# Two more pairs mixed with tokens on partitions, one unit more in the first batch, and one o stage a step forward

## Chip, cores and metric

One NeuronCore of a Trainium2 chip runs the whole kernel. The metric is the device time of one execution in microseconds, and a kernel is judged by several executions. Most executions of one kernel agree within some tenths of a per cent here, but single ones are 1 to 3% longer. Such a run is set aside as slow where it lies over 1.5% above the fastest of its kernel. Times inside a profile (start times, lengths) are counted from the start of the profiled execution, whose span is some 2 us shorter than its device time.

## The reference, cut to what matters

```python
# q, k, v: (B=4, H=8, S=768, D=64); sort_net: (B, H, 8, 8); block = 96
P = sort_net
for _ in range(5):                                   # Sinkhorn: rows and columns in turn
    P = exp(P - max(P)); P = P / rowsum; P = P / colsum
k_sorted = einsum('bhij,bhjcd->bhicd', P, k_b)       # mix the 8 blocks of 96 tokens
v_sorted = einsum('bhij,bhjcd->bhicd', P, v_b)
attn = softmax(q_b @ k_sorted_b.T / sqrt(D))         # within a block
x = (attn @ v_sorted_b)                              # -> (3072, 512), heads side by side
out = ((x @ w_a) * (x @ w_b)) @ w_out                # 512 -> 1536 -> 512
```

## The kernel before

Two heads make a pair; a batch has four pairs (`HP = 4`), so pairs 0 to 3 belong to the first batch, 4 to 7 to the second and so on to 15. The feed-forward part of one batch runs while the attention of the next is prepared between its steps. The attention is cut into units: `c` mixes k and v of a pair, `s` makes scores and exponentials, `o` multiplies with v and turns the result for the feed-forward part. Results of matmuls stand in buffers of a memory called PSUM (the pools `psA` and `psF`) until ScalarE or VectorE has copied them out. A unit stands in a list, and `paced` spreads the list of a batch evenly over the feed-forward steps (the first batch's list here has 18 steps, of about 1.3 us each).

There are two ways of mixing. The old one puts features on partitions at once and takes 24 half-array matmuls; the other leaves tokens on partitions, takes four full matmuls, and then has the DMA crossbar turn the result and GpSimd put it in order:

```python
def stage_k(g):                       # old way; stage_v is alike
    mix = psA.tile([P, 2, 512], FP32, tag="A", name="mix")
    ...
    mix_mms(g, "k", ...)              # 12 matmuls of 128x128, half the array each
    nc.scalar.copy(out=kTs[g % HP] in block order, in_=mix)

def plain(g):
    return g >= 2 * HP + 2            # pairs 10 to 15 take the other way

def stage_plain(g, what, engines):
    ...
    for e in range(2):
        nc.tensor.matmul(mix[:, e, 0:W], lhsT=s_all[:, 2 * g + e], rhs=src2[:, e], ...)
    ...                               # copies mix to nat (bf16)
    nc.sync.dma_start_transpose(out=turned, in_=nat...)     # the crossbar turn

def stage_q(g):                       # q is turned by the crossbar as well, for all pairs from 6 on
    qT = qtp.tile([P, NCH, P], BF16, tag="qTf", name="qTf", bufs=4)
    nc.sync.dma_start_transpose(out=qT, in_=st[g, "qc"]...)
    st[g, "qT"] = qT

def return_v(g):                      # and v back to tokens on partitions
    nc.sync.dma_start_transpose(out=vss[g % NBUF]..., in_=vTs[g % HP]...)
```

All these turns go through one queue, in the order in which they are asked for. Loads of k, v and q go through another; the loads of a later pair are asked for by GpSimd, and a one-element copy called a gate stands before them, so that GpSimd can't ask before something else is finished:

```python
def c_(g):
    ...
    else:                             # a pair mixed the old way
        if g > HP:
            return_v(g)
        if g >= 2 * HP - 2 and g != 2 * HP - 1:
            nc.gpsimd.tensor_copy(out=gate, in_=kTs[g % HP][0:1, 0:1])
            load_later(g)             # loads pair g + 2

def paced(ab, po, units, spare, last):
    steps = ab + po
    total = len(steps) - 2 * spare
    main, done = len(units) - last, 0
    for now, step in enumerate(steps, 1):
        step()
        while done < main and done * total < now * main:
            units[done]()
            done += 1
        ...
```

`c6` asks for the loads of pair 8 (k, v and q, 192 KB each), behind a gate on the k that `c6` itself has just mixed.

The softmax here doesn't subtract the row's maximum and nothing guards it: scores larger than these inputs give would overflow.

## Time and profile before

| | before |
|---|---|
| runs before the prediction | 239.97 us (239.78 to 241.39) |
| span of the profiled run | 238.2 us |
| TensorE busy | 231.5 us, 97% |

The engine shares, the chain and the DMA rows that carry the bound are in the prediction. The first view lists where TensorE waited (in all, times, the longest, in us); the start-up's rows are left out:

```profile
PE pf L362 <- DMA w_b_sb<-in_moe_w_b_dram: 0.5, 1, 0.5
...
PE o_ps L236 <- DVE xp L242: 0.2, 1, 0.2
```

The second is GpSimd's own timeline around the load of pair 8 (start, length, what; in brackets an idle time before it and what ended it):

```profile
50.49 3.96 POOL L153 TENSOR_TENSOR s_all<-mask,p_col 128x1024 bf16<-128x1024 bf16 x2
54.43 0.18 POOL L589 COPY gate<-kT 1x1 bf16<-1x1 bf16 x1
54.93 0.76 POOL L96 DMA_DIRECT2D k<-in_k_dram  x1 [0.32 <-PE pf L362]
```

The third has two transfers asked for at about that time (issued from a queue, how many, us from issue to landing): the turn of q of pair 7, asked for at 52.55, and the load of k of pair 8, asked for at 54.93.

```profile
qTf<-qc SPq DMA_TRANSPOSE x1, 9.5
...
k<-in_k_dram POOLq DMA_DIRECT2D x1, 192.0 KB, 7.8
```

The reader is to see that the load of pair 8 is asked for at 54.93, which is 2.4 us after the turn of q7, and that the turn takes 9.5 us and lands at 62.05. Score stage `s7` starts at 65.43 and doesn't wait for it.

### The profile page before, as it was taken

The numbers are of one execution on the slowest core, as the hardware profiler recorded it, in microseconds if no ns is written. First come the engines' busy times: TensorE is split into PE (matmuls) and PEld (weight loads), VectorE is DVE, ScalarE is ACT, GpSimd is POOL, SyncE is SP. The second block draws the span as 40 slices with busy tenths as digits, with TensorE's granted clock in tenths as the row PEclk, the third lists the DMA queues.
The fourth block names the chain that finished last, engine by engine and source line by source line (L and its number), as shares of the span: only waits on it lengthen the run. The fifth ranks groups of instructions, "written<-read, shape, count | busy, mean of one in ns | idle before, by whom it ended". The sixth has DMA issues, their size and how long they took to land.

```text
span 238.2 us, 5168 instructions
## 1 busy us (share of the span) xinstructions
PE 231.5 (97%) x2064; PEld 138.2 (58%) x2074; DVE 108.5 (46%) x256; ACT 101.4 (43%) x189; POOL 70.4 (30%) x97
## 2 busy tenths in 40 slices
PE   7999999999999999999999999999999999999994
PEld 7776566666554565666555465656554566565442
DVE  7795566546543333465415243645444243444110
ACT  3696543665430366554530366355500234333001
POOL 8786248765010355162420533420000000000000
PEclk9999999999999999999999999999999999999999
DMA  5999999999998999579996999970434300000132
GB/s 76 203 198 193 158 192 201 204 199 189 129 173 169 190 165 170 106 121 168 146 174 172 189 195 143 132 145 4 77 81 128 125 0 3 0 0 3 59 117 88
DMA packets 65703, 30.88 MB, mean 130 GB/s; under 512 B 42512, under 2 KB 62736, under 8 KB 65680
## 3 DMA queue, kind: packets, MB, share of 16 engines
q0 software_dynamic: 20944, 14.16, 42.8%
q1 hardware_dynamic: 44592, 16.33, 37.6%
q8 instruction: 16, 0.26, 0.5%
q10 hardware_dynamic: 144, 0.07, 0.1%
q14 instruction: 7, 0.06, 0.1%
HBM read 28.32 MB, written 6.29 MB: 145 GB/s over the span
## 4 chain that ended last, share of the span: by engine, by line
PE 86%; DMA 5%; DVE 4%; POOL 1%; issue 1%; ACT 1%; DVEq 0%
PE pf L362 51%; PE po L407 24%; DMA w_b_sb<-in_moe_w_b_dram 5%; PE o_ps L236 3%; PE sc L332 2%; PE mix L175 2%; PE mix L303 2%; PE po L392 1%; DMA p_nat<-in_sort_net_dram 1%; POOL w_a_sb L107 1%; DVE csum L461 1%; ACT p_nat L439 1%; DVE xp L242 1%; DVE p_nat L459 0%; POOL s_all L153 0%
## 5 line engine op out<-in xcount | busy, mean ns | idle before, releaser
L383 DVE TENSOR_TENSOR hT<-a_sb,pf 128x384 bf16<-128x384 bf16 x95 | 52.5, 553 | 73.8 <-PE pf L362 44.0
L362 PE MATMUL pf<-xT,w_a_sb 128*128 128x384 bf16 x380 | 78.0, 326 | 0.0
L362 PE MATMUL pf<-xT,w_b_sb 128*128 128x384 bf16 x380 | 77.5, 326 | 0.5 <-DMA w_b_sb<-in_moe_w_b_dram 0.5
L382 ACT CAST a_sb<-pf 128x384 bf16<-128x384 f32 x95 | 45.4, 479 | 61.2 <-PE pf L362 38.2
L407 PE MATMUL po<-w_out_sb,hT 128*128 128x512 bf16 x266 | 61.0, 379 | 0.5
L362 PEld LDWEIGHTS <-w_b_sb 128*128 128x128 bf16 x384 | 37.4, 98 | 25.6 <-DMA w_b_sb<-in_moe_w_b_dram 1.0
L362 PEld LDWEIGHTS <-w_a_sb 128*128 128x128 bf16 x384 | 35.3, 98 | 22.5
L407 PEld LDWEIGHTS <-hT 128*128 128x128 bf16 x276 | 26.3, 98 | 30.1
L161 ACT COPY o_sb<-po 128x512 f32<-128x512 f32 (+1 forms) x13 | 7.5, 577 | 48.9 <-PE po L407 47.5
L163 DVE COPY o_sb<-po 128x512 f32<-128x512 f32 (+1 forms) x12 | 7.9, 658 | 38.7 <-PE po L407 34.1
L337 ACT ACTIVATE eT<-sc 96x768 bf16<-96x768 f32 x24 | 18.0, 802 | 5.1 <-PE sc L332 5.0
L242 DVE TENSOR_TENSOR xp<-o_ps,rec 96x512 bf16<-96x512 f32 x24 | 15.9, 684 | 0.3
L319 POOL COPY kT<-turned 128x768 bf16<-128x768 bf16 x6 | 5.0, 826 | 35.6 <-DMA turned<-nat 31.2
L96 POOL DMA_DIRECT2D k<-in_k_dram x16 | 11.6, 724 | 4.9 <-DMA w_a_sb<-in_moe_w_a_dram 2.7
L96 POOL DMA_DIRECT2D v<-in_v_dram x16 | 11.5, 722 | 4.8 <-DMA w_b_sb<-in_moe_w_b_dram 3.1
L251 POOL COPY qc<-q 128x768 bf16<-128x768 bf16 x10 | 8.4, 841 | 13.8 <-DMA q<-in_q_dram 13.8
L236 PEld LDWEIGHTS <-eT 96*128 96x128 bf16 x256 | 10.3, 97 | 3.4 <-DVE xp L242 0.6
L236 PE MATMUL o_ps<-vs,eT 96*128 96x65 bf16 x256 | 11.3, 193 | 0.3 <-DVE xp L242 0.2
L161 ACT CAST nat<-mix 128x768 bf16<-128x768 f32 (+1 forms) x12 | 7.7, 638 | 4.2 <-PE mix L303 3.0
L96 POOL DMA_DIRECT2D q<-in_q_dram x12 | 8.7, 724 | 2.4 <-DMA w_a_sb<-in_moe_w_a_dram 1.2
L167 PE MATMUL heat<-warm 128*128 128x128 bf16 x84 | 7.8, 268 | 1.3 <-DVE warm L77 1.3
L240 DVE RECIPROCAL rec<-o_ps 96x8 f32<-96x8 f32 x32 | 5.5, 188 | 5.3 <-PE o_ps L236 5.3
(87 smaller groups left out, 154.1 us busy)
## 6 DMA issues: line engine op xcount, KB each, us to landing
out_dram<-o_sb SPq DMA_DIRECT2D x17, 256.0 KB, 2.2
k<-in_k_dram POOLq DMA_DIRECT2D x16, 192.0 KB, 5.9
v<-in_v_dram POOLq DMA_DIRECT2D x16, 192.0 KB, 6.6
q<-in_q_dram POOLq DMA_DIRECT2D x12, 192.0 KB, 7.4
w_a_sb<-in_moe_w_a_dram POOLq DMA_DIRECT2D x6, 256.0 KB, 10.6
w_b_sb<-in_moe_w_b_dram POOLq DMA_DIRECT2D x6, 256.0 KB, 12.1
w_out_sb<-in_moe_w_out_dram POOLq DMA_DIRECT2D x3, 512.0 KB, 11.2
out_dram<-o_sb SPq DMA_DIRECT2D x12, 128.0 KB, 2.8
```

The lines of the kernel that those rows point to most:

```text
L96: nc.gpsimd.dma_start(out=to, in_=_ap(t, base, [[W, P], [S * D, 2], [1, W]]))
L161: nc.scalar.copy(out=out, in_=in_)
L163: nc.vector.tensor_copy(out=out, in_=in_)
L167: nc.tensor.matmul(ps[:, 0:cols], lhsT=warm[:, 0:P], rhs=warm[:, 0:cols], start=True, stop=True)
L236: nc.tensor.matmul(o_ps[:, e, i * (D + 1):(i + 1) * (D + 1)], lhsT=eT[:, hf, e, i * BLK:i * BLK + P], rhs=vs[0:BLK, i0 + i, V0 - 1 + e * ( ...
L242: nc.vector.tensor_tensor(out=_ap(xp, i0 * 2 * D, [[nxp * 2 * D, BLK], [D, 2], [2 * D, NBH], [1, D]]), in0=_ap(o_ps, 1, [[1024, BLK], [511 ...
L251: nc.gpsimd.tensor_copy(out=qc.rearrange("p c e d -> p e c d"), in_=loaded[g][2].rearrange("p e (c d) -> p e c d", c=NCH))
L337: nc.scalar.activation(out=eT[:, hf, :, 0:HB], in_=sc[0:BLK, :, 0:HB], func=AF.Exp, scale=float(scale))
L362: nc.tensor.matmul(pf[:, 0:HW], lhsT=w_sb[:, kc, m * P:(m + 1) * P], rhs=x_cols(b, kc, t), start=(kc == 0), stop=(kc == KA - 1))
L382: nc.scalar.copy(out=a_sb, in_=pf[:, 0:HW])
L383: nc.vector.tensor_mul(out=hT[:, m, t * HW:(t + 1) * HW], in0=a_sb, in1=ab[1][:, 0:HW])
L407: nc.tensor.matmul(held["po"], lhsT=hTs[b][:, m, c * P:(c + 1) * P], rhs=w_out_sb[:, m, :], start=(m == 0), stop=(m == KO - 1))
```

## The change

The intent: pairs 8 and 9 are mixed the cheaper way too. Since the other way takes longer from mixing to use, `c8` is drawn into the first batch, and its v is returned at once; the loads of pairs 9 and 10 now wait for the last turned o stage of the second batch. Apart from that, the first o stage of the first batch's second half comes one step sooner.

```diff
     def plain(g):
-        return g >= 2 * HP + 2
+        return g >= 2 * HP
@@ c_
-                if g >= 2 * HP - 2 and g != 2 * HP - 1:
+                if g == 2 * HP - 2:
                     nc.gpsimd.tensor_copy(out=gate, in_=kTs[g % HP][0:1, 0:1])
                     load_later(g)
@@ o_
-            if g == 2 * HP - 1:
-                nc.gpsimd.tensor_copy(out=gate, in_=xT_of(g // HP)[0:1, HP - 1, 0:1])
-                load_later(g)
@@ the lists
-        plan(0, "c4", "s4", "c5", "s5", "c6", "o4", "s6", "c7", "o5", "s7", "o6", "o7")
-        plan(1, "c8", "s8", "c9", "s9", "c10", "o8", "c11", "o9", "s10", ...
+        plan(0, "c4", "s4", "c5", "s5", "c6", "o4", "s6", "c7", "o5", "s7", "o6", "c8", "o7")
+        plan(1, "s8", "c9", "o8", "c10", "s9", "c11", "o9", "s10", ...
@@ what follows a unit of the plain kind
+                if g == 2 * HP:
+                    after[n + 1].append(lambda g=g: return_v(g))
+                    after[n + 1] += [lambda g=g: nc.gpsimd.tensor_copy(
+                        out=gate, in_=xT_of(1)[0:1, HP - 1, 0:1]),
+                                     lambda g=g: load_later(g - 1), lambda g=g: load_later(g)]
+                    continue
@@ second half of the first batch
-        interleave(steps, units_half(), (0, 0, 1, 0, 1, 2, 1, 1, 1, 2, 1, 0))
+        interleave(steps, units_half(), (0, 0, 1, 1, 0, 2, 1, 1, 1, 2, 1, 0))
```

Thirteen units instead of twelve in the first list mean, through `paced`, that most units come a step sooner; the prediction gives the formula. `c6` is number 5 (counted from 0): it comes after step 7 instead of 8.

More of the change, by code (lines that the diff above doesn't have):

```diff
@@ L617, in plan @@
                 seq.append((b, {"c": c_, "s": s_, "o": o_}[name[0]], int(name[1:])))
-        plan(0, "c4", "s4", "c5", "s5", "c6", "o4", "s6", "c7", "o5", "s7", "o6", "o7")
-        plan(1, "c8", "s8", "c9", "s9", "c10", "o8", "c11", "o9", "s10", "c12", "s11", "o10", "o11",
+        plan(0, "c4", "s4", "c5", "s5", "c6", "o4", "s6", "c7", "o5", "s7", "o6", "c8", "o7")
+        plan(1, "s8", "c9", "o8", "c10", "s9", "c11", "o9", "s10", "c12", "s11", "o10", "o11",
              "c13")
```

## The prediction

> **What bounds the kernel now.** I read the page first (engine shares), then the chain of waits in order of time, then the DMA issues with their times to landing. The page says that TensorE is the bound:
>
> ```profile
> PE 231.5 (97%) x2064; PEld 138.2 (58%) x2074; DVE 108.5 (46%) x256; ACT 101.4 (43%) x189; POOL 70.4 (30%) x97
> PE 86%; DMA 5%; DVE 4%; POOL 1%; issue 1%; ACT 1%; DVEq 0%
> ```
>
> The first line is busy time by engine, the second the chain that ended last. From 27.7 us to the end that chain is one row of TensorE groups with almost nothing between them. So the time can only fall if TensorE gets fewer or cheaper groups, or if one of its few waits goes. The pieces that the change touches (start, length, group):
>
> ```profile
> 27.68 0.82 PE pf L362 x4
> 28.51 0.25 PE o_ps L236 x8
> 53.07 0.79 PE mix L175 x24
> 53.86 1.41 PE pf L362 x8
> 64.20 1.30 PE po L407 x6
> 65.50 0.30 PE sc L332 x8
> 68.89 0.69 DVE o_sb L163
> 69.77 1.26 DVE xp L242 x2
> 71.07 0.42 PE o_ps L236 x8
> 96.46 0.65 PE mix L303 x4
> 97.11 3.90 PE pf L362 x24
> ```
>
> The reader is to see three things. (1) A pair mixed the old way (24 half-array matmuls, L175) costs 0.79 us, and the eight feed-forward matmuls after it 1.41 us. A pair mixed with tokens on partitions (4 full matmuls, L303) costs 0.65, and the matmuls after it 3.90 for 24, that is 1.30 for eight. (2) At 69 to 71 us the chain leaves TensorE: the o stage of pair 7 waits for VectorE to empty PSUM. (3) At 27.68 TensorE has just waited for a weight load. The DMA issues beside this (the last number is us from issue to landing; each is from a narrow window at its issue):
>
> ```profile
> vs<-vT SPq DMA_TRANSPOSE x1, 11.8
> vs<-vT SPq DMA_TRANSPOSE x1, 8.2
> qTf<-qc SPq DMA_TRANSPOSE x1, 2.7
> v<-in_v_dram POOLq DMA_DIRECT2D x1, 192.0 KB, 10.4
> v<-in_v_dram POOLq DMA_DIRECT2D x1, 192.0 KB, 4.5
> ```
>
> They are: v of pair 6 returned, issued at 55.5 (lands 67.3); v of pair 7, issued at 62.15 (lands 70.35); q of pair 8 turned, issued at 69.8; v of pair 8 loaded, issued at 55.7 (lands 66.1); v of pair 9 loaded, issued at 78.0 (lands 82.5). A transfer takes two to four times as long before about 67 us as after it.
>
> **What the Trainium skill says.** "TensorE: Matmul & The Clock Gate", section "Back-to-back issue gap": a warm matmul takes N/2.4 + 2.5 ns. For 384 columns that is 162.5 ns, eight are 1.30 us; for 512 columns 215.8 ns, six are 1.30 us. The trace agrees to the digit (1.30 for eight, 1.30 for six), and four mixing matmuls of 384 columns come out at 0.65 as shown. "TensorEngine Tiling (Array Packing)", section "Key Properties": switching the tiling mode drains TensorE. The trace agrees: 1.41 - 1.30 = 0.11 us after each half-array group, and 0.79 against 12 x 53.3 ns = 0.64 us of streaming (two halves side by side) going in. "DMA: Bandwidth & Descriptors", section "Issuing engines are not separate DMA queues": all DMAs share the same 16 engines and interleave. The trace agrees: with loads running, turns take 8 to 12 us, otherwise 2.7.
>
> **The change part by part.**
> Part 1, the form of mixing of pairs 8 and 9. Each old group costs 0.79 + 0.11 = 0.90 us of TensorE, each new one 0.65. Two pairs: 2 x 0.25 = 0.50 us off the path, 40 matmuls fewer. ScalarE and VectorE empty the same PSUM in the same sizes (0.80, 0.56, 0.48 us each pair): nothing. GpSimd gets four reordering copies of 0.83 us = 3.3 us more and loses two gates, and it is 30% busy. The SP queue gets four more turns. What the path sees is only latency: mix to k ready is about 0.8 (ScalarE copy) + 2.7 (turn at a quiet time) + 0.8 (GpSimd) = 4.3 us, v and its return some 4 more.
>
> Part 2, c8 moves into the first batch. Thirteen units instead of twelve are spread over the same 18 steps, so unit k comes after step floor(18k/13)+1 instead of floor(1.5k)+1. Most units come one step (1.3 us) earlier: o5 after step 12 (was 13), s7 after 13 (was 14), o6 after 14 (was 16); c8 takes step 16 and o7 stays at 17. I place them on the old clock, where step 12 ends at 62.25.
> - o7 no longer follows o6 by one step. In its place come c8's PSUM copies, done about 1.9 us after c8 begins, before o7 wants them at about 2.0 to 2.2. The old wait (PSUM matmuls at 70.48 + 0.25 = 70.73, second half at 71.07) was 0.34 us: gained.
> - s7 follows o5, and o5 now comes right behind the last a-and-b product, whose VectorE product (62.54 to 63.10) stands before o5's reciprocal. Then 2 x (0.20 + 0.69) ends at 64.87, but s7's second half wants the buffer at 62.25 + 0.49 + 1.30 + 0.22 = 64.27: wait 0.6, where the old pair of small waits was 0.2. Lost: about 0.43 with what follows.
> - o6 then comes at 64.9 + 0.25 + 0.1 + 1.30 = 66.55. Its v lands at 67.3 in the old run. Its turn is asked for 0.8 us earlier in the new order (the SP queue stands back to back from 49.7 to 61.4), but its ring was also full of earlier turns and the loads of pair 8 drain until 67.4, so I give it only part of this: landing 66.5 to 67.3. Lost: 0 to 0.8 us, I take 0.4.
> - k and v of pair 8 land by 66.1 and c8 comes at about 69.6 or later: no wait. s8 wants its k at about 82.5, ready by 75: no wait.
>
> Part 3, the first o stage of the second half one step forward. It fills 0.25 us of the wait before 27.68. But the w_b piece for the next two steps lands at 17.86 + 13.0 = 30.86 us (its issue and time to landing), and the matmuls on it started at 30.96 already. So all but 0.03 us of it is waited for again three microseconds later. I count 0.03.
>
> Sum: -0.50 (form) - 0.34 (o7) + 0.43 (s7) + 0.40 (o6 on v6) - 0.03 (first o stage) = -0.04 us. With a little on the good side, since the orders were surely tuned by someone looking at these waits, I predict 239.8 us against 239.97.
>
> **The rivals.**
> Rival A: the waits of s7 and o6 don't come, because v6 lands with its earlier issue and VectorE is ahead. Then the sum is -0.50 - 0.34 - 0.03 = -0.87: 239.1. For it: one to two microseconds of slack are at stake in many places, and the ring of turns begins earlier. Against it: VectorE's order is fixed and the arithmetic for s7 leaves no room.
> Rival B: the turn of v6 takes as long as before from the same drain (67.4 us), or later since nothing else became lighter: +0.8 to +1.0 at o6, sum about +0.5: 240.5. For it: its 11.8 us end just where the loads of pair 8 end.
> Rival C: a wait on the load of pair 9 takes the place of all this. c9 comes after step 3 of the second batch instead of step 5, at about 85.6. The gate for its load stands on GpSimd behind two reordering copies and waits for the last xT of the first batch, which lands at about 77.6 (76.8 before). Then v9 is issued at 78.8 and lands with 4.5 us at 83.3: 2.3 us of slack. If the turns of pair 8 hold that xT up on the SP queue by over 2 us, or the six loads now issued together slow one another, c9 waits one or two microseconds: 241 to 242. Against it: loads issued first have landed first in every window that I read.
> Nothing here reaches 4.8 us, which is 2%.
>
> **Range and chances.** From the best case (239.1) to B (240.5), with 0.2 to 0.3 us for the scatter of the three runs (239.78 to 241.39 before): 238.9 to 240.8 holds it 8 times in 10. Faster by over 2% would need more than TensorE's whole idle time after 27 us, which the chain puts at under 2 us: 0.01. Slower by over 2% needs C and more: 0.02. Within 2%: 0.97.
>
> **What would show it right or wrong.** Part 1: mixing groups of 0.65 us for pairs 8 and 9 too, followed by 1.30 for eight and not 1.41; 24 k-matmuls and 24 v-matmuls fewer under L175. o7: no VectorE piece in the chain before its second half. s7: a wait of about 0.6 us for VectorE's xp before its second half. o6: a wait for the DMA into vs, or none if rival A holds. Part 3: a shorter wait for w_b near 27 us and a new one just before 31 us. Rival C: TensorE idle before the first L303 matmuls on k or v near 85 us. The prediction is wrong if TensorE's gaps between 62 and 72 us change by over 1 us in either direction, or if a gap opens after 80 us where I see none.

## The result

| | before | after |
|---|---|---|
| median of 6 runs | 240.01 us (239.78 to 241.98) | 243.74 us (242.91 to 245.24) |
| ratio of fast runs | | 1.0137 (1.0089 to 1.0184) |
| span of the profiled run | 238.2 us | 241.3 us |

A ratio is the mean time of one kernel's fast runs over that of the other's fast runs of the same rounds, so not quite the ratio of the medians; the bounds are a 95% interval. The kernel became 1.4% slower: inside the class "within 2%", but 2.9 us above the upper end of the predicted range.

The page of the changed kernel, the same two lines that the prediction begins with:

```profile
PE 231.4 (96%) x2034; PEld 136.9 (57%) x2034; DVE 108.9 (45%) x256; ACT 101.7 (42%) x189; POOL 73.0 (30%) x99
...
PE 64%; DMA 25%; DVE 3%; POOL 3%; issue 2%; ACT 1%; DVEq 0%; POOLq 0%
```

TensorE has 30 recorded matmuls fewer (40 were taken out; some matmul records are missing from both traces) and is busy as long as before, but 25% of the chain that ended last now runs through DMAs, where 5% did. TensorE's waits say which; these are the ones after the start-up:

```profile
PE sc L332 <- DMA qTf<-qc: 3.3, 1, 3.3
...
PE mix L303 <- DMA v<-in_v_dram: 0.4, 1, 0.4
```

The chain in order of time (start, length, what) leads through both:

```profile
49.74 2.85 POOL s_all L153 x2
52.59 14.91 DMA qTf<-qc
67.50 0.14 issue
67.64 0.52 PE sc L332 x16
68.16 1.40 PE po L407 x6
69.56 0.49 PE o_ps L236 x16
70.05 2.59 PE po L407 x12
72.64 0.65 PE mix L303 x4
73.29 1.29 PE po L407 x6
...
83.39 5.87 DMA v<-in_v_dram
...
89.31 0.50 PE mix L303 x2
```

Read it backwards from 67.64. `s7` (16 matmuls of L332) starts there, because the turn of q of pair 7 lands only at 67.50. The turn was asked for at 52.59, as in the kernel before (52.55); it took 14.91 us instead of 9.5. Further down, pair 8 is mixed in 0.65 us and followed by 1.29 for six products, so the cheaper form does what it was meant to. At 89.31 the v matmuls of `c9` had to wait for v of pair 9.

How much of the loss is that? From each trace the start of the same piece of TensorE's work:

| piece | before | after | difference |
|---|---|---|---|
| b product in the first batch's second half | 30.96 | 30.94 | -0.02 |
| b product two steps later | 34.29 | 34.42 | +0.13 |
| first product of the second batch | 80.39 | 83.98 | +3.59 |
| mixing of pair 13 | 133.77 | 137.05 | +3.28 |
| last group of products (L392) | 232.10 | 235.37 | +3.27 |

Nearly everything is lost between the second and third row, where the difference grows by 3.46. The sum: 3.29 us of wait at `s7`, in place of the 0.20 that it lost to VectorE before, and 0.65 for `c8`, which moved there, less the 0.34 us step at `o7` that is gone, make 3.40. Later, `c8` and the dearer form of `c9` are saved (0.90 + 0.25). Lost there are 0.55 at `c9` (its v matmuls start 0.87 after its k matmuls instead of 0.32; TensorE's list shows 0.38 of it) and 0.27 at `o9`, which starts at 110.45, 0.92 after the four products before it instead of 0.65: its weight load waits for v of pair 9 to be returned. That makes -0.33, and -0.31 was seen.

So the question is why a turn that was asked for at the same time took 5.4 us longer. What else happened at that time? GpSimd's timeline of the changed kernel:

```profile
49.70 3.96 POOL L153 TENSOR_TENSOR s_all<-mask,p_col 128x1024 bf16<-128x1024 bf16 x2
53.62 0.18 POOL L589 COPY gate<-kT 1x1 bf16<-1x1 bf16 x1
53.77 0.76 POOL L96 DMA_DIRECT2D k<-in_k_dram  x1
```

The load of pair 8 is asked for at 53.77 instead of 54.93. `c6` came a step sooner (its k matmuls start at 51.84 instead of 53.00), so ScalarE's copy of k ends at 52.41 + 0.80 = 53.21 instead of 53.57 + 0.80 = 54.37, and the gate that reads it no longer holds GpSimd. (Part of the 1.16 us is that q of pair 7 came 0.8 us sooner in this run, so that GpSimd was free at 53.66 instead of 54.45. With the old pace this would have changed nothing, because the gate can't fire before 54.37.) The two transfers themselves:

```profile
qTf<-qc SPq DMA_TRANSPOSE x1, 14.9
...
k<-in_k_dram POOLq DMA_DIRECT2D x1, 192.0 KB, 12.0
```

Not only the turn is slower: the load that begins sooner takes 12.0 us instead of 7.8. And here is what the two queues moved from 58 to 62 us (packets, MB, the packets' time as a share of 16 engines; q1 carries the turns, q0 the loads), first before, then after:

```profile
q1 hardware_dynamic: 1546, 0.38, 80.6%
q0 software_dynamic: 310, 0.23, 66.6%
```

```profile
q1 hardware_dynamic: 910, 0.22, 100.4%
q0 software_dynamic: 221, 0.16, 42.1%
```

The kernel before moved 0.38 + 0.23 = 0.61 MB in these 4 us; the changed one moved 0.22 + 0.16 = 0.38 MB, with about as much of the engines' time taken (100.4 + 42.1 = 142.5%, against 80.6 + 66.6 = 147.2%). No queue gained what the other lost: both went slower. The rates of the same 4 us in 40 slices of 0.1 us, before and then after:

```profile
GB/s 79 92 136 253 265 287 292 287 287 161 92 294 441 195 210 179 179 205 64 64 49 79 28 120 189 164 154 233 251 266 246 192 72 23 28 15 8 8 15 15
```

```profile
GB/s 125 266 244 266 90 79 72 77 69 64 92 67 79 74 90 82 105 90 95 72 49 236 108 51 95 69 97 72 74 77 113 77 87 90 84 87 97 108 95 87
```

Before, the queues reach some 180 to 290 GB/s in about half of the slices and have run dry at the end. After, they drag along at some 50 to 110 from 58.4 us on (but for one slice of 236), and still have work at 62.

### The profile page after: what moved, and what is told of

It is laid out like the page before. It is cut to its first block, busy times and chain, and to the rows that moved or that the text cites. A ratio compares the mean times of both kernels' runs of the same rounds, so it can differ in the third digit from the quotient of the medians.

```text
span 241.3 us, 5107 instructions
## 1 busy us (share of the span) xinstructions
PE 231.4 (96%) x2034; PEld 136.9 (57%) x2034; DVE 108.9 (45%) x256; ACT 101.7 (42%) x189; POOL 73.0 (30%) x99
## 4 chain that ended last, share of the span: by engine, by line
PE 64%; DMA 25%; DVE 3%; POOL 3%; issue 2%; ACT 1%; DVEq 0%; POOLq 0%
PE pf L362 36%; PE po L407 22%; DMA qTf<-qc 6%; DMA k<-in_k_dram 5%; DMA w_a_sb<-in_moe_w_a_dram 4%; DMA q<-in_q_dram 3%; DMA v<-in_v_dram 2%; DMA vs<-vT 2%; PE o_ps L236 2%; PE mix L303 2%; POOL s_all L153 2%; PE sc L332 2%; DMA xT<-xp 1%; PE po L392 1%; POOL qc L251 1%
## 5 line engine op out<-in xcount | busy, mean ns | idle before, releaser
L407 PE MATMUL po<-w_out_sb,hT 128*128 128x512 bf16 x276 | 61.9, 379 | 0.0
L319 POOL COPY kT<-turned 128x768 bf16<-128x768 bf16 x8 | 6.6, 830 | 42.6 <-DMA turned<-nat 32.8
L161 ACT CAST nat<-mix 128x768 bf16<-128x768 f32 (+1 forms) x16 | 10.2, 639 | 8.2 <-PE mix L303 6.7
L332 PEld LDWEIGHTS <-kT 64*128 64x128 bf16 x192 | 4.5, 94 | 7.3 <-issue 6.4
```

What stands on the lines that cost most here:

```text
L161: nc.scalar.copy(out=out, in_=in_)
L332: nc.tensor.matmul(sc[:, e, i * BLK:(i + 1) * BLK], lhsT=kT[e * D:(e + 1) * D, blk * BLK:blk * BLK + P], rhs=qT[e * D:(e + 1) * D, :, blk ...
L407: nc.tensor.matmul(held["po"], lhsT=hTs[b][:, m, c * P:(c + 1) * P], rhs=w_out_sb[:, m, :], start=(m == 0), stop=(m == KO - 1))
```

## The experiments

My theory after this: the new pace frees the gate of pair 8's load, the load starts in the middle of the turns, and load and turns slow one another; `s7` pays. The rivals: the new form as such (four more turns in the queue) slows the queue; the order of the units makes `s7` want its q sooner; the first o stage moved something; or the slow profile was chance. Runs sent together share the runs of the kernel before, whose median was 239.95 to 240.00 us in each set.

### The parts one by one

**Only the pace.** The kernel before, with its own twelve units on the steps that they have after the change:

```diff
-                while done < main and done * total < now * main:
+                while done < main and (done * total < now * main if at is None else at[done] <= now):
...
+                  (1, 2, 3, 5, 6, 7, 9, 10, 12, 13, 14, 17) if b == 0 else None)
```

> The kernel before, with the units of the first batch on the steps that the change gives them (most one step of 1.3 us earlier, o6 two), but c8 still in the second batch and mixed the old way. In the changed kernel the turn of q of pair 7 landed at 67.5 us (62.05 before) and s7 waited 3.3 us for it. Theory 1 (the earlier steps let the load of pair 8 start earlier, which collides with the turns): the turn of q7 lands again after 65 us, s7 waits 1 to 3.5 us, time 241.5 to 243.5. Theory 2 (the new form of pairs 8 and 9 is what costs): no wait at s7, time 240 to 240.7, the 0.4 us that I worked out for s7 behind o5.

Measured: 240.75, 244.61, 241.51 and 245.50 us. Two of the four counted as slow (granted clock 0.993 and 0.990) and have no trace; the fast two give a ratio of 1.0034 (0.9990 to 1.0078), which settles nothing. The profile fell on the shortest of the four. In it the load was asked for at 54.44, since q of pair 7 had come 0.7 us later to GpSimd than in the changed kernel, and the turn of q7 landed at 63.90, not after 65 as theory 1 had it; what it does show is the wait for v6 that I had predicted at `o6`, at the place and about half the size:

```profile
66.55 0.67 PE L236 MATMUL o_ps<-vs,eT 96*128 96x65 bf16 x16 [0.19 <-DMA vs<-vT]
```

Whether the pace alone makes the loss is not shown by this run: a difference that only slow runs have is no evidence.

**Only the first o stage.**

```diff
-        interleave(steps, units_half(), (0, 0, 1, 0, 1, 2, 1, 1, 1, 2, 1, 0))
+        interleave(steps, units_half(), (0, 0, 1, 1, 0, 2, 1, 1, 1, 2, 1, 0))
```

> The kernel before with only the first o stage of the second half one step forward. Theory 1 and 2 alike: 239.9 to 240.1, the gap before 27.7 us shorter by 0.25 us and a new one of 0.2 us just before 31 us. If this part upsets the transfers (it asks for a turn of v 1.8 us earlier), the turn of q7 would land late here too and the time be 241 or more.

Measured: 240.49 us (240.16 to 240.64), ratio 1.0006 (0.9979 to 1.0033). The median lies 0.4 us above what I expected, but the ratio shows no difference: this part is worth nothing that can be measured. The run has a second use: it keeps the old pace, and in its profile q of pair 7 came as soon as in the changed kernel (GpSimd's `s_all` starts at 49.70 in both). So it shows what the gate does there:

```profile
54.58 0.18 POOL L589 COPY gate<-kT 1x1 bf16<-1x1 bf16 x1 [0.92 <-ACT kT L285]
55.08 0.76 POOL L96 DMA_DIRECT2D k<-in_k_dram  x1 [0.32 <-PE pf L362]
```

GpSimd stood still for 0.92 us until ScalarE had copied k of pair 6. With the old pace the gate is a brake on the load, whatever GpSimd's own state.

**The change without its pace.** The changed kernel with the first batch's units on the old steps and `c8` put in at 16:

```diff
+                  (1, 2, 4, 5, 7, 8, 10, 11, 13, 14, 15, 16, 17) if b == 0 else None)
```

> The changed kernel with its first-batch units up to s7 on the steps that they had before, o6 at 15, c8 at 16, o7 at 17. Theory 1: the load of pair 8 starts near 54.9 us again, the turn of q7 lands near 62, s7 doesn't wait, time 239 to 240. Theory 2: still 242.5 or more, since pairs 8 and 9 are mixed the new way.

Measured: 240.31 us (239.46 to 240.80), ratio 0.9996 (0.9963 to 1.0030). The loss is gone though both pairs keep the new form. That refutes the rival that the four more turns alone are to blame.

### The load alone

**The new pace, the load after the turn.** The changed kernel, its gate reading the turned q of pair 7 in place of the mixed k of pair 6:

```diff
-                    nc.gpsimd.tensor_copy(out=gate, in_=kTs[g % HP][0:1, 0:1])
+                    nc.gpsimd.tensor_copy(out=gate, in_=st[g + 1, "qT"][0:1, 0, 0:1])
```

> The changed kernel, but the load of pair 8 is gated on the landing of the turn of q7 instead of on k of pair 6. Theory 1 (collision of that load with the turns): q7 lands by 61 us, s7 does not wait for it, time 239 to 240.3; k and v of pair 8 land by 69, in time for c8. If turns are slow for another reason, q7 still lands after 65 us, the load comes later still, c8 waits for it and the time is 243 or more.

Measured: 240.07 us (239.69 to 240.13), ratio 0.9991 (0.9960 to 1.0022). The steps and the form are those of the changed kernel; only the load moved. The order of the units, too, is thus refuted as the cause by itself. So is another rival, that the turn of v of pair 5, asked for sooner with the new pace, holds up the one of q7: it was asked for at 48.44 here and at 48.49 in the changed kernel (49.65 before). Its chain shows what the wait at `s7` is once the turn is on time:

```profile
62.61 0.56 DVE hT L383
63.17 0.19 DVE rec L240 x2
63.35 1.26 DVE xp L242 x2
64.61 0.05 issue
64.66 0.34 PE sc L332 x8
```

`s7`'s second half stands behind VectorE's products of `o5`, which end at 64.61, and starts at 64.66 (the 0.34 beside it is the length of its matmuls). The prediction had worked out 64.87 for VectorE's end. What the wait costs is seen in the length of the whole stage, in the kernel before and then here:

```profile
65.43 0.72 PE L332 MATMUL sc<-qTf,kT 64*128 64x96 bf16 x16
```

```profile
64.23 0.77 PE L332 MATMUL sc<-qTf,kT 64*128 64x96 bf16 x16
```

Undisturbed, the stage takes 0.52 us (at 67.64 in the changed kernel). So it loses 0.20 us to VectorE before and 0.25 here. The wait is real, but only 0.05 of it is new, where the prediction had a loss of 0.43.

The run shows one thing more. The turn of q7 took 9.2 us, although the load of pair 8 was asked for only at 62.16, after it had landed. From 50 to 56 us the load queue moved 0.31 to 0.34 MB in every 2 us, as in the kernel before (0.31 to 0.35): these were loads asked for earlier, among them the three pieces of `w_out` with 512 KB each, asked for from 43.12 on. So most of the turn's long way is not owed to pair 8's load, but to what stood in the queues before.

**The same on the kernel with the pace alone.**

```diff
-                    nc.gpsimd.tensor_copy(out=gate, in_=kTs[g % HP][0:1, 0:1])
+                    nc.gpsimd.tensor_copy(out=gate, in_=st[7, "qT"][0:1, 0, 0:1] if g == 6 else
+                                          kTs[g % HP][0:1, 0:1])
```

> The kernel of the pace alone (240.8 to 245.5 in four runs), with the load of pair 8 gated on the turn of q7. Theory 1: the late landings go, all runs within 239.8 to 240.8, s7 waits only 0.3 us for VectorE. Rival (the pace of the turns): still some runs over 242.

Measured: 240.51, 248.13, 240.29 and 240.37 us; the second counted as slow (granted clock 0.986) and has no trace, so I can't say what it was. Fast runs: 1.0011 (0.9987 to 1.0034). The turn of q7 landed at 61.09 (63.90 with the pace alone). Since both kernels had slow runs, the times don't tell them apart.

**The load much sooner, with the old pace.** Two versions of the kernel before, with the load of pair 8 asked for between or ahead of GpSimd's two `s_all` products and no gate:

```diff
         for g in range(2, 4):
+            if g == 3:            # the second version: g == 2
+                load_pair(2, 0)
             spread(nc.gpsimd, p_col, g * 8, 8)
```

> The kernel before with nothing of the change, only the load of pair 8 sent some 2.4 us earlier (at 52.5 us, between two of GpSimd's products, without its gate). So far the turn of q7 landed at 67.5, 63.9, 62.05 and 61.1 us where that load began at 53.8, 54.4, 54.9 and 55.0, and at 61.6 where it waited for the turn. Theory 1 (the load's start against the turns): the turn lands at 65 us or later, s7 (65.4 at the earliest here) waits up to 3 us, time 240.5 to 243. Rival (the turn of v5, asked for a microsecond sooner in the new pace, holds q7 up): no effect, 239.8 to 240.4, q7 lands near 62.

> The same, the load of pair 8 some 4.4 us earlier (at 50.5 us, before both products). Theory 1: the turn of q7 lands later still than with 2.4 us, time 241 to 244, unless the load is then mostly through before the turns get going, when it would land as before. Rival: 239.8 to 240.4.

Measured: 240.26 us (239.90 to 240.67) and 240.35 us (239.97 to 240.69), ratios 1.0006 and 1.0009. The load now starts 3.4 and 5.3 us before the one of the kernel before, and nothing is lost. So "a sooner load is a worse load" is wrong as a rule. The turn of q7 did get later (63.84 and 64.03 us instead of 62.05), but not late enough for an `s7` that starts at 65.29 and 65.39 with the old pace.

**A tuned version**: the late load, the old steps, `c9` moved and v of pair 9 returned sooner.

```diff
-                after[n + late].append(lambda g=g: return_v(g))
+                after[n + (1 if g == 9 else late)].append(lambda g=g: return_v(g))
...
+                  ((1, 2, 4, 5, 7, 8, 10, 11, 13, 14, 15, 16, 17),
+                   (1, 4, 6, 9, 11, 14, 17, 19, 22, 25, 27, 30), None, None)[b])
```

> The changed kernel with the load of pair 8 gated on the turn of q7, the first-batch units up to s7 on their old steps (o6 at 15), c9 one step later and the return of v of pair 9 right after its reordering. All waits seen in the gated kernel should go: 0.34 us at s7, 0.2 to 0.4 at c9, 0.1 at o9. What is left of the change is the form's 0.5 us and o7's 0.34: time 239.1 to 239.5, ratio to before 0.996 to 0.998. If the form's gain is not real, 239.8 or more.

Measured: 239.99 us (median of 240.38, 245.34, 239.47, 239.54, 241.29 and 239.60; the second counted as slow), ratio of the fast runs 0.9994 (0.9963 to 1.0024). A miss: with the wait of `c9` taken away, TensorE's list has a new one, 0.9 us at `c11` for its v.

### Which start of the load is the bad one?

By now a late load was harmless, a much sooner one as well, and the one in between was bad. That left open whether the pace, the form or the load's start alone does it. So: the changed kernel once more, the changed kernel with the load on either side of the bad start, and the kernel before with nothing but its gate taken out.

**The changed kernel again.**

> The changed kernel unaltered, once more with a profile, on the chip of the next three. If the late turn of q7 is its rule and not a chance of the one trace: the turn of q7 lands at 66 us or later, s7 waits over 2 us, 242.5 to 245 in every run. If a chance: s7 waits less than 1 us in this trace and some run is under 241.

Measured: 243.84 us (241.53 to 244.10), ratio 1.0139 (1.0104 to 1.0173). The loss is no chance of one measurement: it comes back at the same size, and the score stages' waits for turned q are there again, 3.1 us in two waits: 1.29 at `s6` and 1.80 at `s7`. The two queues crawled again as well: from 58 to 62 us they moved 0.23 + 0.04 MB.

**The new pace, the load 3 us sooner**: asked for ahead of both `s_all` products, no gate.

```diff
         pair_q(2 * HP - 1)
+        load_pair(2, 0)
         for g in range(2, 4):
...
-                if g == 2 * HP - 2:
-                    nc.gpsimd.tensor_copy(out=gate, in_=kTs[g % HP][0:1, 0:1])
-                    load_later(g)
```

> The changed kernel with the load of pair 8 sent 4 us earlier (49.6 us instead of 53.8), before the turns get going. In the kernel before this made the turn of q7 land at 64.0 and the time stayed. Theory 1b (only a load that starts while the turns of v5, q7 and v6 fill the ring stretches them to 67): lands near 64, s7 waits under 0.6 us, 239.8 to 241. Rival (the new pace by itself stretches the turns, wherever the load stands): lands at 66 or later, 242.5 or more.

Measured: 240.32 us (239.93 to 241.01), ratio 1.0012 (0.9992 to 1.0032). The same pace and form as the changed kernel, a sooner load, and most of the loss is gone. Something is still paid: the turn that comes late now is that of an earlier v, and TensorE's list has

```profile
PE o_ps L236 <- DMA vs<-vT: 1.6, 2, 0.9
```

**The new pace, the load 3 us later**: gate and load moved behind `o4`, the gate reading the last element of its product.

```diff
-                if g == 2 * HP - 2:
-                    nc.gpsimd.tensor_copy(out=gate, in_=kTs[g % HP][0:1, 0:1])
-                    load_later(g)
@@ o_
+            if g == HP:
+                nc.gpsimd.tensor_copy(out=gate, in_=st[g, "xp"][0:1, NB - 1, 1, D - 1:D])
+                load_later(g + 2)
```

> The changed kernel with the load of pair 8 sent about 2.5 us later (near 56.3, gated on the output of the first crossbar pair's o stage). Theory 1b: the turn of q7 is further through when the load comes, lands by 63.5, s7 waits only the 0.34 us for VectorE, 239.8 to 240.8. Rival: 242.5 or more.

Measured: 239.16 us (239.00 to 239.66), ratio 0.9968 (0.9955 to 0.9981). Not only is the loss gone: this version is 0.3% faster than the kernel before, which is small, but outside its interval. GpSimd's timeline shows the new gate at work, and the DMA view shows the same 4 us as above, 58 to 62:

```profile
56.52 0.18 POOL L603 COPY gate<-xp 1x1 bf16<-1x1 bf16 x1 [2.65 <-DVE xp L242]
57.01 0.77 POOL L96 DMA_DIRECT2D k<-in_k_dram  x1 [0.31 <-PE pf L362]
```

```profile
q1 hardware_dynamic: 2116, 0.53, 125.1%
q0 software_dynamic: 85, 0.06, 10.4%
```

The turns move 0.53 MB, more than twice the 0.22 of the changed kernel; the load gets through afterwards.

**The kernel before without that gate.** Form, units, order and pace of the kernel before; nothing holds the load of pair 8 any longer:

```diff
-                    nc.gpsimd.tensor_copy(out=gate, in_=kTs[g % HP][0:1, 0:1])
+                    if g > 2 * HP - 2:
+                        nc.gpsimd.tensor_copy(out=gate, in_=kTs[g % HP][0:1, 0:1])
```

> The kernel before at its own pace, only the gate of pair 8's load on k of pair 6 taken out, so that the load begins as soon as GpSimd is through with its products, at 53.5 us (or 54.4 where q of pair 7 landed late). If the load's start alone makes the late turn: q7 lands at 66 or later, s7 (65.4) waits 0.6 to 2 us, some runs over 241. If it needs the new pace too: q7 lands by 64, no wait at s7, 239.8 to 240.6.

Measured: 244.04, 242.01, 242.73 and 239.98 us. The first was profiled; it counts as slow, since it lies over 1.5% above the fastest of the four, at a granted clock of 1.0. The fast three give 1.0055 (0.9997 to 1.0113), so the times leave it open whether this edit costs anything. The one trace, of the slow run, has the same mark as the changed kernel, though not one line of its form or pace is changed; TensorE's wait, and the two queues from 58 to 62 us:

```profile
PE sc L332 <- DMA qTf<-qc: 2.7, 2, 2.5
```

```profile
q1 hardware_dynamic: 929, 0.23, 129.8%
q0 software_dynamic: 81, 0.06, 12.4%
```

The turn of q7 took 15.0 us there. Everything up to the load is some 1.1 us later in that run (the turn of q6 was asked for at 48.01 instead of 46.85), so start times on the clock can't be set beside those of other runs; counted from the turn of q6, the load started at 6.9 us, like the changed kernel's. One slow run can't show that the load's start is enough in the old kernel too; it only agrees with it.

### A better version

**The next load sooner.** The change on the old steps, the load of pair 9 asked for in `c8` already instead of behind the last turned o stage:

```diff
                 stage_q(g)
+                if g == 2 * HP:
+                    load_later(g - 1)
...
-                                     lambda g=g: load_later(g - 1), lambda g=g: load_later(g)]
+                                     lambda g=g: load_later(g)]
```

> The changed kernel on the old steps of the first batch (240.3 median before, with a wait of 0.1 to 0.4 us of c9 for v of pair 9) and with the load of pair 9 sent when c8 is through instead of behind the gate, some ten microseconds earlier. c9 no longer waits; all waits of TensorE known so far are gone or as before, and the form's 0.5 us and o7's 0.34 stay: 239.2 to 239.6, ratio to before 0.997 to 0.999. If the earlier load disturbs the turns of pair 8 and the last xT of the batch, 240 or more.

Measured: 239.17 us (five runs from 239.08 to 239.20, one of 241.31), ratio 0.9980 (0.9953 to 1.0006).

**Both together**: the load of pair 8 behind `o4`, and that of pair 9 in `c8`.

> The changed kernel with the load of pair 8 gated on o4's output (as in e11: 239.2) and the load of pair 9 sent ahead of pair 8's reordering (as in e12). If the two add up: 238.8 to 239.2, the only wait left on TensorE's path the 0.34 us at s7. If e11 had already no wait at c9, nothing is added: 239.0 to 239.4.

Measured: 239.72 us (239.09 to 240.60), ratio 0.9979 (0.9944 to 1.0014). No sum of the two gains can be seen. (The edits are the two shown above.)

**The best one again**, unaltered.

> The kernel of e11 again, on another chip perhaps, in five rounds: 239.0 to 239.6 in nearly all runs, ratio to before 0.995 to 0.999. If e11 was a lucky chip, 239.8 or more or a run over 241.

Measured: 239.31 us (239.02 to 240.73), ratio 0.9973 (0.9935 to 1.0011). Of the ten runs of this version, nine lie between 239.0 and 239.7, against a median of 239.95 to 239.97 of the kernel before in the same rounds: it is faster by about 0.3%, though the interval of this second study alone includes no difference. Its chain runs through TensorE almost throughout again:

```profile
64.55 0.34 PE sc L332 x8
64.89 1.40 PE po L407 x6
66.30 0.49 PE o_ps L236 x16
66.79 2.59 PE po L407 x12
69.38 0.65 PE mix L303 x4
70.03 1.29 PE po L407 x6
71.33 0.49 PE o_ps L236 x16
71.82 9.07 PE po L407 x42
```

`c8` at 69.38 stands between `o6` and `o7`, and neither waits for anything: the gain that the change was after.

### All starts in one table

To compare runs whose clocks are shifted, each time is counted from the moment at which the turn of q of pair 6 is asked for, the first of the row of turns concerned. Each row is one profiled run; the last column is the median time of that kernel's fast runs.

| kernel | load of pair 8 asked for | turn of q7 landed | median of fast runs, us |
|---|---|---|---|
| before, load ahead of both products | 2.88 | 17.31 | 240.35 |
| after, load ahead of both products | 3.77 | 17.18 | 240.32 |
| before, load between them | 4.84 | 17.20 | 240.26 |
| before without the gate (profiled run slow) | 6.87 | 21.39 | 242.01 |
| **after** | 6.98 | 20.70 | 243.74 |
| **after, again** | 6.98 | 20.60 | 243.84 |
| before, new pace (two of four runs slow) | 7.56 | 17.02 | 241.13 |
| **before** | 8.08 | 15.20 | 240.01 |
| after, old steps and next load sooner | 8.27 | 14.49 | 239.17 |
| before, first o stage moved | 8.29 | 14.34 | 240.49 |
| after, old steps | 8.29 | 14.35 | 240.31 |
| after, load behind `o4`, second study | 9.82 | 14.48 | 239.31 |
| after, load behind `o4` | 9.98 | 14.35 | 239.16 |
| after, load behind `o4`, next load sooner | 10.01 | 14.33 | 239.72 |
| before, new pace, load behind the turn | 14.87 | 14.36 | 240.37 |
| tuned | 15.18 | 14.62 | 239.60 |
| after, load behind the turn | 15.42 | 14.82 | 240.07 |

Where the load comes at 8.27 us or later, the turn lands at 14.3 to 14.8 whatever else is changed. Where it comes before 5 us, it lands at about 17.2. Only between, near 6.9, does it land at 20.6 to 21.4: twice in the changed kernel, and once in the kernel before without its gate, there in a slow run. What is shown by fast runs is this: in the changed kernel, with form, order and pace as they are, moving the load to either side takes the loss away. In the changed kernel `s7` wants it at 64.3, which is 17.5 on this scale. A landing at 17.2 costs nothing at `s7`, and one at 20.7 costs 3.2 us, which is the 3.3 of TensorE's list.

## Why the prediction was wrong

**Form of mixing: right.** 0.65 us for pairs 8 and 9 (but for the wait inside `c9`), then 1.29 or 1.30 per group, and the old groups gone. (The section "Back-to-back issue gap", which the prediction names for N/2.4 + 2.5 ns, gives this for an isolated matmul and about 131 ns at 512 columns for a stream in a real kernel. Here it is a stream, and 1.30 us for six are 217 ns each: the measurement decides for the formula.)

**`o7`: right.** No VectorE piece stands before its second half any longer, in the changed kernel or in the better version.

**First o stage: right.** It stands at 26.51, the b products that come after start at 30.94 instead of 30.96 (I had written that all but 0.03 us would be waited for again), and alone it measured as nothing. The next b product waits a little too, for a later piece of `w_b`: 34.42 instead of 34.29. So 0.13 us were lost here instead of 0.03 gained.

**`s7`: the step that failed.** The prediction gave it a wait of 0.6 us for VectorE and no other, and took the landing of its q from the old trace without saying so. Instead `s7` waits 3.29 us for the turn of q7, which took 14.9 us instead of 9.5 because the load of pair 8 started at 53.77 instead of 54.93; with that load moved away (to 57.01, or to behind the turn) the loss is gone. The gap that the prediction named as a sign that it is wrong, over 1 us between 62 and 72, is this one. The VectorE wait shows only in the versions whose turn is on time, and there costs 0.25 us where the old kernel lost 0.20: mis-sized as well, 0.05 in place of 0.43. The mechanism was missing from the working, not only mis-sized: I had listed that most units come a step sooner, and followed this for `o5`, `s7` and `o6`, that is, for TensorE's order. In `c6` I followed it for the turn of v6, but not for the gate, which lets go of a load. And I had read that a turn takes two to four times as long beside loads, and then treated the landings themselves as fixed, apart from v6. That reading was too simple as well: it compares turns that stand in a row behind others with one that stands alone. The run with the load behind the turn shows 9.2 us without pair 8's load, beside older loads; how much of that is the row and how much the older loads is not separated.

**`o6` on v6 (0 to 0.8 us, taken as 0.4): right in kind where it can be seen.** 0.19 us with the pace alone, 0.3 us in the second run of the changed kernel. In the first it is hidden, since `s7` before it came 3 us late. Its turn was asked for 0.12 us sooner (55.38 instead of 55.50), not the 0.8 that I had worked out.

**Rival C: right in kind, smaller.** I had given it one or two microseconds. The gate for pair 9's load fired at 81.86, its v was asked for at 83.39 and took 5.87 us, and `c9` waited 0.38 and lost 0.55 in all; `o9`, later, lost 0.27 to the return of that v.

**The sum.** Put what was measured into the prediction's sum: 3.29 - 0.20 = 3.09 for the 0.43 of `s7`, nothing for `o6` (hidden), +0.13 for the first o stage with the wait after it, and 0.55 + 0.27 for rival C. Then it is -0.50 - 0.34 + 3.09 + 0.13 + 0.82 = +3.20, against 3.27 at the last group of products, 3.1 between the two profiled spans and 3.73 between the medians. The range failed because its upper end was made of single waits that I had seen; a moved transfer was not among the ways in which it could go.

**What stays open.** Why a load that begins just there makes both queues crawl, while one that begins 2 us sooner or 1.3 us later does not: the traces show low rates at full busy time, not what happens inside the DMA engines. That the scatter of the kernel with the pace alone comes from q of pair 7 reaching GpSimd sooner or later is my reading of its one profile, not shown. The slow runs of three versions (pace alone, pace with the load behind the turn, tuned) have no trace. The load of pair 8 is three transfers, k, v and q; which of them matters was not tried.

## What to carry to other kernels

A gate that looks like protection of a buffer also sets the time of a transfer: when units change places, list for each of them not only the work that it does but the loads and turns that it lets go. A landing time read from an old trace holds only as long as nothing beside that transfer moves; where two streams share the DMA engines, look at what starts within some microseconds of it. Then try several starts for the load and measure each: here a gate moved by 3 us turned a loss of 1.4% into a gain of 0.3%, while one that waited until the turn had landed only came out even.

## What the Trainium skill lacked or had wrong

- "Advanced Engine Details and Errata", section "X-Bar Transpose (TRN2)", says that crossbar transposes are as fast as regular DMAs, and gives 350 to 400 GB/s. In the best stretch that I read (the load behind the turn, 60.8 to 62 us, nothing but turns) they moved 0.34 MB at 284 GB/s. That is no less than loads alone reached there (0.40 MB at 202 GB/s from 48 to 50 us), so the comparison isn't contradicted, but the figure wasn't reached. Beside loads, in the changed kernel from 58 to 62 us, all queues together moved 101 GB/s. A turn asked for at a quiet time took 2.7 us; the turn of q7, which stood behind other turns and beside older loads, took 8.4 to 9.5 us in the good cases and 14.7 and 14.9 in the two runs of the changed kernel. The measurement decides: a turn can't be reckoned at that one rate.
- "DMA: Bandwidth & Descriptors", section "Issuing engines are not separate DMA queues", says that DMAs of different issuers interleave on the same 16 engines. That agrees with the turns and loads in flight together here. It doesn't say what becomes of the sum, which fell: from 58 to 62 us it was 0.61 MB before, 0.59 with the load behind `o4`, but 0.38 and 0.27 in the two runs of the changed kernel (and 0.29 in the slow run of the kernel without the gate).
- I know of no page that says that the start of a load within a row of turns decides this: in the profiled runs, a load 7.0 us after the turn of q6 went with a landing of q7's turn at 20.6 to 20.7 us, one at 4.8 us or sooner with 17.2 to 17.3, and one at 8.27 us or later with 14.3 to 14.8.
- "TensorEngine Tiling (Array Packing)", section "Key Properties", says that a change of tiling mode drains TensorE, without a figure: here a group of eight products beside half-array matmuls took 0.11 us longer (1.41 against 1.30), and this is gone for pairs 8 and 9 with the new form. That the drain is what takes it is the page's word; the trace shows only the time.
